# Four edits to a tuned kernel of attention, a gated convolution and DFT mixing: a frequency from a number per token, earlier bits, later sigmoids, other banks

## The chip, the cores and the metric

The kernel runs on one core of a Trainium2 chip. The core has a matrix engine (TensorE, PE in the profile; its weight loads are PEld), VectorE (DVE), ScalarE (ACT) and GpSimd (POOL), each with its own instruction queue, and SyncE (SP), whose queue issues most of the DMAs. The engines meet only at semaphores. The metric is the device time of one execution in microseconds (us).

## The reference, cut to what matters

```python
# 1. attention: 2 batches, 8 heads, 768 tokens, 64 per head
q_bits = (q @ proj > 0); k_bits = (k @ proj > 0)      # 6 bits per token
mask = bucket(q_bits)[..., :, None] == bucket(k_bits)[..., None, :]
scores = where(mask, q @ k.T / 8, -1e9)
x = softmax(scores) @ v                               # -> (2, 768, 512)
# 2. gate: causal convolution of 5 taps per channel
x = (sigmoid(conv(x, conv_w)) * (x @ w_val)) @ w_out
# 3. mixing by DFT along the tokens and along the channels
u = x + real(fft(fft(x, axis=1), axis=2))
un = (u - mean(u)) / sqrt(var(u) + 1e-6)
out = u + maximum(un @ w_ch1, 0) @ w_ch2              # 512 -> 2048 -> 512
```

## The kernel before

Every matmul operand is split into a high and a low part of 32-bit floats, and a product is three matmuls (high x high, high x low, low x high) that add up in one bank of PSUM. The weights arrive as 64-bit floats and are converted on the chip from their two words each (`from64`, `words_split`): masks and shifts on VectorE, a scaling on ScalarE, and at the end a low part (line 156 on GpSimd when `spare`, line 158 on VectorE otherwise) and a high part (line 163, ScalarE). All work stands in each engine's queue in the order of the program; nothing reorders it (`manual_schedule`). A tile waits for the last reader of the memory that it takes over.

**Attention** is a loop over n, 96 blocks of 128 queries (8 pairs of heads, 12 blocks each) and two more steps to drain it. In step n TensorE transposes block n (`p_transpose`), makes the scores of block n + 3 (`scores`) and multiplies with the values for the block pair before (`pv`). VectorE limits the scores (`clamp`, line 549) and makes the low part of the transposed block (`p_low`, line 586); ScalarE does the exponential (`expo`, 556) and the high part (`p_high`, 582). There is one tile of two banks for scores (pool `pss`), so the scores of a block wait for the clamp of the one before; there are two for transposes (`pst`), and one bank each in `psm` and `pso`. `start` prepares the first pair of heads. The second head's projected bits are made by `project(1, ...)` in step 0 and thresholded by `start_bits` (line 440) later in that step; `bits_place` copies them by two DMAs into the operands of the scores.

In the last steps (NT = 96) the value matmuls of the gate for the first half of batch 0 come early (`val_matmul`, line 216, into tiles `early`), the weights of w_out are converted in the gaps, `norm_transpose` (636, 639) turns the reciprocal sums, `x_split` makes the parts of the second half of x, and `sigmoid` makes the gates. A one-element activation (line 878) loads ScalarE's table for sigmoids. `pv_out` of the last block copies its result twice on ScalarE (610, 612), GpSimd adds (615) and multiplies with the norm (696). Then come 48 value matmuls (`late`) and the stage `mixing`.

**Mixing.** The first part finishes the gates, with even and odd sums over the tokens (`even_odd`, line 1002) on VectorE. Then a loop over 12 jobs (batch, symmetry s, block kt) runs through `own` (product with w_out), `fold` (the sum or difference of columns d and 512 - d), `turn` (transposes by TensorE, 1126 and 1128, and their two parts) and `along_d` (the DFT along the channels against `tab`, 1145), each one job behind the other. `fold` leaves the column d = 0 out. So `turn` also transposes the first 128 columns of y, and `along_d` adds two matmuls with a table `first` that is 2 in its row 0 and 0 elsewhere: y[:, 0] reaches all 258 outputs. `both` does the DFT along the tokens (`mixed`, 1165), adds it to y (`total`, 1171 to 1176) and lets GpSimd write u (1186). The centering of batch 0 (`center`) and its transposes stand beside the jobs of batch 1.

**Channel mixing** loops over g, 2 x 16 blocks of 128 of the 2048 hidden channels: `first` (1275) makes the hidden block, `second` (1287) adds to six accumulators `acc0` to `acc5`, one for each block of tokens. For g = 0 and 1 the hidden blocks go through the banks of accumulators 2 to 5. `channel_split(h)` converts half h (w_ch1 for even h, w_ch2 for odd) of block h // 2 and starts the load of half h + 2. Halves 0 and 1 are converted within the mixing, half 2 at the start of the channel mixing.

Of the kernel before, what the change touches and what calls it, by code (L numbers as in the profile page):

```python
# [17 lines left out]
P = 128  # L18
# [30 lines left out]
def dft_tables():  # L49


    d = np.arange(1, DM // 2 + 1)
    l = np.arange(NL)
    ang = 2.0 * np.pi * ((d[:, None] * l[None, :]) % DM) / DM
    cs = 2.0 * np.stack([np.cos(ang), np.sin(ang)], 0)
    cs[0, -1] = 1.0 - 2.0 * (l % 2)
    cs[1, -1] = 0.0
    ch, cl = split12(cs)
    wide = np.stack([ch, cl], 1).reshape(2, 2, 2, P, NL).transpose(3, 0, 1, 2, 4)

    j = np.arange(HS)
    k = np.arange(HS)
    ang = 2.0 * np.pi * ((j[:, None] * k[None, :]) % S) / S
    c = np.cos(ang)
    s = -np.sin(ang)
    c[0, 1::2] = 0.0
    c[1::2, 0] = 0.0
    s[:, 0] = 0.0
    t = np.stack([c, s], 0)
    th, tl = split12(t)  # L70
    seq = np.stack([th, tl], 1).reshape(2, 2, HS // P, P, HS).transpose(3, 0, 1, 2, 4)

    odd = np.zeros((P, 2, P), np.float32)
    odd[0, 0, 1::2] = 1.0
    odd[1::2, 1, 0] = 1.0
    return (
        np.ascontiguousarray(wide, dtype=np.float32),
        np.ascontiguousarray(seq, dtype=np.float32),
        odd,
    )  # L80
# [22 lines left out]
def block_kernel(  # L103
# [23 lines left out]

    def from64(words_of, raw, dst_h, dst_l, half=False, parts=P, spare=False):

        n = raw.shape[1]  # L130
        words = raw.bitcast(I32).rearrange("p (n two) -> p n two", two=2)
        lo, hi = words[:, :, 0], words[:, :, 1]
        a, e, g = (words_of(n, x)[:parts] for x in "aeg")
        b = 4 if half else 3

        def fold(x):
            return x.rearrange("p (c f) -> p c f", c=dst_h.shape[1]) if len(dst_h.shape) == 3 else x

        def s0():
            nc.vector.tensor_scalar(a, hi, 0x7FFFFE00, None, op0=ALU.bitwise_and)  # L140

        def s1():
            nc.scalar.activation(a, a, AF.Relu, scale=8.0, bias=col[:parts, b : b + 1])  # L143

        def s2():
            nc.vector.tensor_scalar(g, hi, 0x1FF, 15, op0=ALU.bitwise_and, op1=ALU.logical_shift_left)
            nc.vector.scalar_tensor_tensor(g, lo, 17, g, op0=ALU.logical_shift_right, op1=ALU.bitwise_or)

        def s3():
            nc.vector.scalar_tensor_tensor(a, hi, -(2 ** 31), a, op0=ALU.bitwise_and, op1=ALU.bitwise_or)  # L150
            nc.vector.tensor_scalar(e, a, -(2 ** 23), None, op0=ALU.bitwise_and)  # L151

        def s4():
            if spare:
                nc.scalar.mul(g.bitcast(F32), g, 2.0 ** -35)
                nc.gpsimd.tensor_tensor(dst_l, fold(g.bitcast(F32)), fold(e.bitcast(F32)), op=ALU.mult)  # L156
            else:
                nc.vector.scalar_tensor_tensor(
                    dst_l, fold(g), 2.0 ** -35, fold(e.bitcast(F32)), op0=ALU.mult, op1=ALU.mult
                )  # L160

        def s5():
            nc.scalar.copy(dst_h, fold(a.bitcast(F32)))

        return [s0, s1, s2, s3, s4, s5]
# [128 lines left out]
    def attention(es):  # L294
# [133 lines left out]
        def two_banks():  # L428
            return [psm.tile([P, HS], F32, tag="m", name="bp"), pso.tile([P, HS], F32, tag="o", name="bp")]
# [86 lines left out]
        def start_bits(bps):  # L516
            bits = st[0]["bits"] = ap1.tile([P, S], F32R, tag="bits", name="bits")
            for a in range(2):
                bit(bits[64:, :], slice(64, P), a, bps)
            bits_place(0, 1)  # L520
            values(0, 1)

# [205 lines left out]
        def conv_weights():  # L728
            cwr, cwh, cwl, cw = cws
            
            def words_of(n, x):
                c0 = (2 + "aeg".index(x)) * P
                return conv_tmp[:, c0 : c0 + n].bitcast(I32)

            steps = from64(words_of, cwr, cwh, cwl, parts=20)
# [33 lines left out]

        tail = []  # L770
        convs = [(b, c, i) for b, c in pairs[: NPR - 1] for i in range(9)]
        start()
        NT = 12 * NPR
        for n in range(NT + 2):
# [6 lines left out]
            if n == 0:  # L781
                bps = project(1, two_banks())
            if n + 3 < NT:
# [19 lines left out]
            if n == 0:  # L803
                start_bits(bps)
            if p + 1 < NPR:
# [10 lines left out]
            if i == (5 if last else 9) and 1 <= p < NPR:  # L816
                norm_mul(p - 1)
            if n == NT - 1:
                xsplit[0, 1] = tuple(
                    ap0.tile([P, R, QB], F32R, tag=x, name="x01").rearrange("p r (c t) -> p (r c t)", c=2)  # L820
# [3 lines left out]
                for c in range(NC):  # L824
                    x_split(0, 1, c, nc.vector)
            if n in (NT - 1, NT):
                norm_transpose(NPR - 1, n - NT + 1)
            if n == NT + 1:
# [40 lines left out]
            if p == 5 and i in (1, 3, 5, 7):  # L869
                x_split(0, 0, i // 2)  # L870
            if NT - 3 <= n < NT + 1:
                c = n - NT + 3
                if c % 2 == 0:
                    early = (pst if c else pss).tile([P, 2, 512], F32, tag="t" if c else "s", name="early")
                tail.append(early[:, c % 2, :HS])
                val_matmul(0, 0, c, tail[c])
            if n == NT - 3:
                nc.scalar.activation(warm, warm, AF.Sigmoid)
            if NT - 2 <= n < NT:
                for x in range(2):  # L880
                    sigmoid(0, 2 * (n - NT + 2) + x)
                if n == NT - 1:
                    g_again(0, slice(0, NC))
            if n >= NT - 2:
                gate(0, 0, n - NT + 2, tail[n - NT + 2])
        out_tile(2)
# [13 lines left out]
    u, mu, uth, utl, rstd = [], [], [], [], []  # L900
    wq, wch, wraw, wst = None, [], {}, []

# [29 lines left out]
    def channel_words(n, x):  # L932
        return wq.tile([P, n], I32, tag=f"cv{x}", name="cv", bufs=1)

    def channel_split(h):
        if h < 2 * NF:
            f, i = divmod(h, 2)
            run(from64(channel_words, wraw[h], *wch[f][2 * i : 2 * i + 2], spare=True))
            channel_load(h + 2)
# [24 lines left out]
    def mixing(es):  # L964
# [11 lines left out]
        tab = mp.tile([P, 2, 2, 2, NL], F32R, name="tab")  # L976
        first = mp.tile([P, NL], F32R, name="first")
        odd = mp.tile([P, 2, P], F32R, name="odd")
# [103 lines left out]
        g_again(1, slice(2, 3))  # L1082
        nc.gpsimd.memset(f32(first), 0.0)
        nc.gpsimd.memset(f32(first)[0:1, :], 2.0)
        for s in range(2):
# [36 lines left out]
        def turn(b, s, kt, part):  # L1122
            n = 2 if part else 3
            pt = bank()
            for i, x in enumerate([folds[b, s, kt, part][:, i * P : (i + 1) * P] for i in range(2)]):
                nc.tensor.transpose(pt[:, i * P : (i + 1) * P], x, ident)
            if n == 3:
                nc.tensor.transpose(pt[:, 2 * P : 3 * P], ys[b, s, kt][:, 0:P], ident)
            fh, fl = turned[b, s, kt, part] = [
                m2.tile([P, 3, P], F32R, tag=f"f{x}", name="ft", bufs=2)[:, :n] for x in "hl"  # L1130
            ]
            src = pt[:, : n * P].rearrange("p (n t) -> p n t", n=n)
            nc.scalar.copy(fh, src)
# [4 lines left out]
        def along_d(b, s, kt, part):  # L1138
            fh, fl = turned[b, s, kt, part]
            ops = [(x[:, i, :], tab[:, part, w, i, :]) for x, w in ((fh, 0), (fh, 1), (fl, 0)) for i in range(2)]  # L1140
            if part == 0:
                ops += [(x[:, 2, :], first) for x in (fh, fl)]
            pa = psum()
# [57 lines left out]
        for i in range(len(jobs) + 2):  # L1201
# [45 lines left out]
    def channel(es):  # L1247
# [9 lines left out]
        for f in order[4:]:  # L1257
            wch[f] = channel_tiles(fp, f)
        channel_split(2)

# [40 lines left out]

        both = []
        for g in range(B * NF + 1):
            if g < B * NF:
# [7 lines left out]
            if g > 0:  # L1312
# [55 lines left out]
```

## Time and profile before

| what | us |
|---|---|
| median of 3 runs | 631.28 (631.07 to 631.45) |
| the profiled execution | 631.46 |
| its span, first to last instruction | 629.7 |
| TensorE busy | 616.0 (98%) |
| VectorE, ScalarE, GpSimd busy | 445.9, 356.4, 263.9 |

The profile is of one execution. The share of an engine's busy time is a mean over stages: attention lies from 0 to 259 us, the mixing to 353, the channel mixing behind it. Times of a row count from the span's start.

### The profile page before, as it was taken

What the parts mean: (1) busy time and instruction counts of PE and PEld (TensorE: products, weight loads), DVE (VectorE), ACT (ScalarE), POOL (GpSimd) and SP (SyncE); (2) the same over time, 40 slices, a digit from 0 to 9 for tenths busy, and PEclk for the clock granted to TensorE, in tenths of its full rate; (3) what the DMA queues carried; (4) which work ended last, traced back from release to release, by engine and by line L of the source; (5) the groups of instructions that cost most, each with busy time, mean ns of one, the idle gap of its engine ahead of it and who ended that gap; (6) DMA issues with size and microseconds to landing.
All of it is one profiled execution on the core that took longest, in us unless ns stands there. A gap on an engine that the chain in (4) does not pass through costs nothing.

```text
span 629.7 us, 10559 instructions
## 1 busy us (share of the span) xinstructions
PE 616.0 (98%) x3794; PEld 576.7 (92%) x3794; DVE 445.9 (71%) x847; ACT 356.4 (57%) x713; POOL 263.9 (42%) x289
## 2 busy tenths in 40 slices
PE   7999999999999999999999899999999999999997
PEld 7899999999999998998899889999998999999996
DVE  5998989898989897797769788889885411111113
ACT  5887989898989797844525255555665111011121
POOL 7133478777888788792350533322331000000000
PEclk9999999999999999999999999999999999999999
DMA  6857585847566530251100144344440200000002
GB/s 155 198 126 169 128 184 123 177 121 167 141 143 158 152 90 13 72 227 68 33 35 1 35 128 132 114 130 134 133 134 1 100 1 1 0 1 1 1 1 100
DMA packets 54060, 60.25 MB, mean 96 GB/s; under 512 B 28936, under 2 KB 42332, under 8 KB 53752
## 3 DMA queue, kind: packets, MB, share of 16 engines
q1 hardware_dynamic: 53272, 56.02, 34.1%
q0 software_dynamic: 432, 3.55, 1.5%
q8 instruction: 30, 0.49, 0.3%
q14 instruction: 22, 0.18, 0.1%
q10 hardware_dynamic: 304, 0.01, 0.0%
HBM read 33.98 MB, written 3.15 MB: 59 GB/s over the span
## 4 chain that ended last, share of the span: by engine, by line
PE 88%; DVE 7%; ACT 2%; issue 1%; DMA 1%; POOL 0%; SPq 0%; DVEq 0%; ACTq 0%; POOLq 0%
PE pf L1275 20%; PE acc L1287 20%; PE sp L537 10%; PE op L597 9%; PE ptp L574 8%; PE ps L1105 5%; PE ps L216 3%; PE ps L1165 3%; PE bp L414 2%; PE ps L1145 2%; DVE ptl L586 2%; DVE sd L549 2%; PE late L216 1%; PE ptp L669 1%; PE ptp L649 1%
## 5 line engine op out<-in xcount | busy, mean ns | idle before, releaser
L1287 PE MATMUL acc<-w,hid 128*128 128x512 f32 x576 | 137.0, 390 | 0.0
L1287 PEld LDWEIGHTS acc<-w,hid 128*128 128x128 f32 x576 | 107.4, 188 | 19.7
L1278 DVE SCALAR_TENSOR_TENSOR hid<-pf,hid 128x384 fp32r<-128x384 f32 x60 | 32.2, 555 | 120.1 <-ACT hid L1277 120.1
L549 DVE TENSOR_SCALAR_CACHE_REDUCE sd<-sp 128x768 f32<-128x768 f32 x96 | 90.9, 948 | 14.7 <-PE sp L537 14.0
L1275 PE MATMUL pf<-uth,w 128*128 128x384 f32 x480 | 94.8, 338 | 0.2 <-POOL w L156 0.2
L586 DVE TENSOR_TENSOR ptl<-ptp,pth 128x768 fp32r<-128x768 f32 x96 | 91.4, 952 | 3.2 <-ACT pth L582 3.2
L537 PE MATMUL sp<-qk 128*128 128x384 f32 x384 | 90.9, 359 | 2.8 <-DVE sd L549 1.5
L1277 ACT ACTIVATE hid<-pf 128x384 fp32r<-128x384 f32 x60 | 28.0, 488 | 113.9 <-PE pf L1275 113.9
L582 ACT CAST pth<-ptp 128x768 fp32r<-128x768 f32 x96 | 77.3, 805 | 26.8 <-PE ptp L574 10.0
L556 ACT ACTIVATE sd<-sd,nm 128x768 f32<-128x768 f32 x96 | 90.7, 945 | 2.7 <-DVE sd L549 2.7
L1275 PEld LDWEIGHTS pf<-uth,w 128*128 128x128 f32 x480 | 85.7, 188 | 2.9 <-POOL w L156 0.6
L156 POOL TENSOR_TENSOR w<-cv 128x512 fp32r<-128x512 f32 x32 | 41.4, 1294 | 89.6 <-DVE cv L151 76.6
L574 PE MATMUL ptp<-ident,sd 128*128 128x128 f32 x576 | 78.6, 272 | 0.2 <-ACT sd L556 0.2
L597 PE MATMUL op<-ptl,v 128*128 128x256 f32 x288 | 73.6, 285 | 0.3 <-DVE ptl L586 0.3
L597 PE MATMUL op<-pth,v 128*128 128x256 f32 x288 | 73.5, 281 | 0.2 <-ACT xc L610 0.2
L537 PEld LDWEIGHTS sp<-qk 128*128 128x128 f32 x384 | 62.4, 189 | 6.4 <-DVE sd L549 3.9
L574 PEld LDWEIGHTS ptp<-ident,sd 128*128 128x128 f32 x576 | 65.9, 141 | 1.1 <-ACT sd L556 0.5
L615 POOL TENSOR_TENSOR xm<-xc,xs 64x256 f32<-64x256 f32 x48 | 35.5, 740 | 68.5 <-DMA xs<-xc 36.0
L597 PEld LDWEIGHTS op<-ptl,v 128*128 128x128 f32 x288 | 54.1, 188 | 1.6 <-DVE ptl L586 0.5
L597 PEld LDWEIGHTS op<-pth,v 128*128 128x128 f32 x288 | 54.2, 188 | 0.6 <-ACT xc L610 0.4
L1275 PE MATMUL pf<-utl,w 128*128 128x384 f32 x240 | 52.1, 338 | 0.0
L143 ACT ACTIVATE cv<-cv,col 128x512 int32<-128x512 int32 x32 | 23.2, 725 | 48.1 <-DVE cv L140 48.1
(214 smaller groups left out, 1047.1 us busy)
## 6 DMA issues: line engine op xcount, KB each, us to landing
raw<-in_moe_w_ch_dram SPq DMA_DIRECT2D x32, 512.0 KB
qk<-ht SPq DMA_DIRECT2D x60, 192.0 KB
qk<-lt SPq DMA_DIRECT2D x30, 192.0 KB
rqk<-in_q_dram SPq DMA_DIRECT2D x16, 192.0 KB
rqk<-in_k_dram SPq DMA_DIRECT2D x16, 192.0 KB
rv<-in_v_dram SPq DMA_DIRECT2D x8, 384.0 KB
out_dram<-o SPq DMA_DIRECT2D x12, 256.0 KB
xs<-xc SPq DMA_DIRECT2D x47, 64.0 KB
```

Source lines behind the costliest of these rows:

```text
L156: nc.gpsimd.tensor_tensor(dst_l, fold(g.bitcast(F32)), fold(e.bitcast(F32)), op=ALU.mult)
L537: nc.tensor.matmul(sp[:, a, :HS], q2[i][:, m, qi * P : (qi + 1) * P], k2[i][:, m, a * HS : (a + 1) * HS], start=m == 1, stop=m == 0,)
L549: nc.vector.tensor_scalar(sd[n].rearrange("p (a c) -> p a c", a=2), sp[:, :, :HS], CLAMP, None, op0=ALU.min, op1=ALU.min, accum_out=st[p][ ...
L556: nc.scalar.activation(sd[n], sd[n], AF.Exp, bias=st[p]["nm"][:, i : i + 1], scale=-1.0, accum_out=st[p]["sums"][:, i : i + 1],)
L574: nc.tensor.transpose(tp[:, r // 3, c0 : c0 + P], sd[n][:, r * P : (r + 1) * P], ident)
L582: nc.scalar.copy(p_parts(n)[0], tp)
L586: nc.vector.tensor_tensor(lo, tp, f32(ho), op=ALU.subtract)
L597: nc.tensor.matmul(po[kb], v3[:, r, c0 : c0 + P], pt[kb][x][:, r, :], start=r == 0 and x == 0, stop=r == R - 1 and x == 1,)
L615: add[kb] = lambda: nc.gpsimd.tensor_tensor(st[p]["xm"][mr, blk * QB : (blk + 1) * QB], xc[mr, :], xs[mr, :], op=ALU.add)
L1275: nc.tensor.matmul(pf[:, :HS], w[:, c, :], x[:, c, cs], start=n == 0, stop=n == 3 * NC - 1)
L1278: nc.vector.scalar_tensor_tensor(hl[:, cs], pf[:, :HS], 0.0, f32(hh)[:, cs], op0=ALU.max, op1=ALU.subtract)
L1287: nc.tensor.matmul(acc, x[:, ts_], w, start=f == 0 and n == 0, stop=f == NF - 1 and n == 2)
```

## The change

1. *d = 0 as a number per token.* The third transpose of `turn`, the table `first` (and the two GpSimd instructions that fill it) and its two matmuls in `along_d` go. Instead the eviction of `along_d` adds y[:, 0] per token: ScalarE's copy becomes an Identity with a bias, VectorE's subtraction an instruction with three operands. A factor of two moves from the table of the channels to those of the tokens.
2. *Second head's bits ahead of a clamp.* In step 0 `start_bits` comes straight behind `project(1, ...)`, ahead of clamp(3). `values(0, 1)` stays where it was.
3. *Sigmoids behind the last copies.* The table load moves from step 93 to 94, the sigmoids of batch 0 from steps 94 and 95 to 95 and 96, the gates with them. In step 95 the early value matmuls and the first `norm_transpose` come ahead of `x_split`.
4. *Banks and first conversion.* Two accumulators are made ahead of the first hidden block, so that all tiles of the channel mixing take other banks. Half 2 of the weights is converted without `spare`: its steps 0 to 2 ahead of `both(1, 0)`, step 3 behind it, the last two at the start of the channel mixing. `from64` asks for its destination only when it writes, since that tile exists only then.

```diff
@@ dft_tables
-    cs = 2.0 * np.stack([np.cos(ang), np.sin(ang)], 0)
-    cs[0, -1] = 1.0 - 2.0 * (l % 2)
+    cs = np.stack([np.cos(ang), np.sin(ang)], 0)
+    cs[0, -1] = 0.5 - (l % 2)
...
-    t = np.stack([c, s], 0)
+    t = 2.0 * np.stack([c, s], 0)
...
-    odd[0, 0, 1::2] = 1.0
-    odd[1::2, 1, 0] = 1.0
+    odd[0, 0, 1::2] = 2.0
+    odd[1::2, 1, 0] = 2.0
@@ start_bits
             bits_place(0, 1)
-            values(0, 1)
@@ attention
+        def val_early(n, early):
+            c = n - NT + 3
+            tail.append(early[:, c % 2, :HS])
+            val_matmul(0, 0, c, tail[c])
...
             if n == 0:
-                bps = project(1, two_banks())
+                start_bits(project(1, two_banks()))
             if n + 3 < NT:
                 clamp(n + 3, scores(n + 3))
...
             if n == 0:
-                start_bits(bps)
+                values(0, 1)
...
             if n == NT - 1:
+                early = pst.tile([P, 2, 512], F32, tag="t", name="early")
+                val_early(n, early)
+                norm_transpose(NPR - 1, 0)
                 xsplit[0, 1] = tuple(
...
-            if n in (NT - 1, NT):
-                norm_transpose(NPR - 1, n - NT + 1)
+            if n == NT:
+                norm_transpose(NPR - 1, 1)
...
-            if NT - 3 <= n < NT + 1:
-                c = n - NT + 3
-                if c % 2 == 0:
-                    early = (pst if c else pss).tile([P, 2, 512], F32, tag="t" if c else "s", name="early")
-                tail.append(early[:, c % 2, :HS])
-                val_matmul(0, 0, c, tail[c])
             if n == NT - 3:
+                early = pss.tile([P, 2, 512], F32, tag="s", name="early")
+            if NT - 3 <= n < NT + 1 and n != NT - 1:
+                val_early(n, early)
+            if n == NT - 2:
                 nc.scalar.activation(warm, warm, AF.Sigmoid)
-            if NT - 2 <= n < NT:
+            if NT - 1 <= n < NT + 1:
                 for x in range(2):
-                    sigmoid(0, 2 * (n - NT + 2) + x)
-                if n == NT - 1:
+                    sigmoid(0, 2 * (n - NT + 1) + x)
+                if n == NT:
                     g_again(0, slice(0, NC))
-            if n >= NT - 2:
-                gate(0, 0, n - NT + 2, tail[n - NT + 2])
+            if n >= NT - 1:
+                for c in range(n - NT + 1, n - NT + (2 if n < NT + 1 else 3)):
+                    gate(0, 0, c, tail[c])
@@ mixing
-        nc.gpsimd.memset(f32(first), 0.0)
-        nc.gpsimd.memset(f32(first)[0:1, :], 2.0)
...
-            if n == 3:
-                nc.tensor.transpose(pt[:, 2 * P : 3 * P], ys[b, s, kt][:, 0:P], ident)
...
-            if part == 0:
-                ops += [(x[:, 2, :], first) for x in (fh, fl)]
...
-            nc.scalar.copy(ah[:, part, slot, :], pa[:, :NL])
-            nc.vector.tensor_tensor(al[:, part, slot, :], pa[:, :NL], f32(ah)[:, part, slot, :], op=ALU.subtract)
+            high, low = ah[:, part, slot, :], al[:, part, slot, :]
+            if part:
+                nc.scalar.copy(high, pa[:, :NL])
+                nc.vector.tensor_tensor(low, pa[:, :NL], f32(high), op=ALU.subtract)
+            else:
+                y0 = ys[b, s, kt][:, 0:1]
+                nc.scalar.activation(high, pa[:, :NL], AF.Identity, bias=y0)
+                nc.vector.scalar_tensor_tensor(
+                    low, pa[:, :NL], y0, f32(high), op0=ALU.add, op1=ALU.subtract
+                )
...
-        for kt in range(3):
+        wnext.extend(channel_steps(2, spare=False))
+        run(wnext.pop(0) for _ in range(3))
+        both(1, 0)
+        wnext.pop(0)()
+        for kt in range(1, 3):
             both(1, kt)
@@ channel
-        channel_split(2)
+        run(wnext)
+        channel_load(4)
...
+        last = [tile_a(t) for t in range(2)]
...
                 if f == 0:
-                    acc = [tile_a(t) for t in range(6)]
+                    acc = (last if b == 0 else [tile_a(t) for t in range(2)]) + [tile_a(t) for t in range(2, 6)]
```

## Rows read from the trace of the kernel before

**Rows 1.** The page's busy time, share of the span and instructions of each engine.

```profile
PE 616.0 (98%) x3794; PEld 576.7 (92%) x3794; DVE 445.9 (71%) x847; ACT 356.4 (57%) x713; POOL 263.9 (42%) x289
```

**Rows 2.** Chain that ended last, 0 to 36 us: start, duration (us), what.

```profile
35.44 0.17 DVE sd L549
```

**Rows 3.** Chain that ended last, whole span.

```profile
377.00 4.24 PE pf L1275 x24
```

**Rows 4.** Timeline, 12 to 40 us: start, duration, engine, line, idle before and its releaser.

```profile
16.60 0.96 DVE L549 TENSOR_SCALAR_CACHE_REDUCE sd<-sp 128x768 f32<-128x768 f32 x1 [1.07 <-PE sp L537]
...
18.45 1.29 DVE L440 TENSOR_SCALAR bits<-bp,col 64x384 fp32r<-64x384 f32 x2
...
19.20 0.55 PE L388 MATMUL tp<-ident,rqk 128*128 128x128 f32 x3 [0.60 <-DVE bits L440]
...
20.80 0.97 PE L537 MATMUL sp<-qk 128*128 128x384 f32 x4 [0.40 <-DVE sd L549]
```

**Rows 5.** Timeline, 246 to 260 us, the end of attention.

```profile
246.13 1.28 ACT L878 ACT_TABLE_LOAD   x1
...
247.53 0.78 ACT L582 CAST pth<-ptp 128x768 fp32r<-128x768 f32 x1
...
250.71 0.37 ACT L278 CAST qk<-cvp 128x256 fp32r<-128x256 f32 x1 [2.05 <-DVE qk L275]
...
251.23 0.52 PE L636 MATMUL rp<-ident,rb 128*128 128x128 f32 x3 [0.65 <-ACT qk L278]
...
255.61 0.55 PE L636 MATMUL rp<-ident,rb 128*128 128x128 f32 x3 [0.45 <-ACT rs L639]
...
258.79 0.86 PE L216 MATMUL late<-x,wvh 128*128 128x384 f32 x4
...
259.44 0.36 ACT L612 COPY xs<-op 64x256 f32<-64x256 f32 x1
```

**Rows 6.** Windows: length, busy us of PE, PEld, DVE, ACT, POOL; clock, DMA share, GB/s.

```profile
250.98:257.64 6.66, 5.62 (x34) 5.19 (x35) 3.85 (x7) 6.63 (x14) 3.75 (x4) 1.00 0.30 91
262.00:284.00 22.00, 22.00 (x128) 22.00 (x127) 20.77 (x37) 11.32 (x25) 20.43 (x24) 1.00 0.50 186
332.00:340.00 8.00, 8.00 (x47) 6.91 (x46) 7.32 (x19) 2.51 (x7) 0.00 (x0) 1.00 0.01 2
```

**Rows 7.** Timeline, 262 to 290 us: start of the mixing.

```profile
262.68 1.02 DVE L1002 TENSOR_TENSOR gt<-g,late 128x384 f32<-128x384 f32 x2 [0.91 <-POOL xT L696]
...
288.63 0.57 ACT L1115 COPY y<-ps 128x512 f32<-128x512 f32 x1
...
289.86 0.41 PE L1126 MATMUL pw<-ident,fold 128*128 128x128 f32 x2
```

**Rows 8.** Groups of TensorE instructions by line and form: busy us, mean ns.

```profile
L1145 PE MATMUL ps<-first,ft 128*128 128x258 f32 x16 | 3.2, 283 | 0.0
...
L1128 PE MATMUL pw<-ident,y 128*128 128x128 f32 x8 | 2.2, 272 | 0.0
```

**Rows 9.** Chain that ended last, 280 to 373 us.

```profile
290.27 0.11 PE pw L1128
...
293.19 0.98 PE ps L1145 x8
```

**Rows 10.** Groups of ScalarE instructions by line.

```profile
L1316 ACT ACTIVATE u<-u,mu 128x512 f32<-128x512 f32 x12 | 8.6, 717 | 0.0
```

**Rows 11.** Timeline, 343 to 376 us: from the mixing to the channel mixing.

```profile
349.27 7.88 POOL L1186 TENSOR_TENSOR u<-y 128x512 f32<-128x512 f32 x6 [22.07 <-DVE y L1176]
...
354.05 1.64 PE L1275 MATMUL acc<-uth,w 128*128 128x384 f32 x8 [0.94 <-DVE y L1176]
354.48 1.51 DVE L146 TENSOR_SCALAR cv<-raw 128x512 int32<-128x512 int32 x1
...
360.33 0.97 PE L1275 MATMUL acc<-uth,w 128*128 128x384 f32 x4 [0.32 <-POOL w L156]
...
360.69 0.42 DVE L146 TENSOR_SCALAR cv<-raw 128x512 int32<-128x512 int32 x1
```

More of the change, by code (lines that the diff above doesn't have):

```diff
@@ L126, in pool, with from64 @@
         return es.enter_context(tc.tile_pool(name=name, bufs=bufs, reuse_waits="tile", **kw))
-    def from64(words_of, raw, dst_h, dst_l, half=False, parts=P, spare=False):
+    def from64(words_of, raw, dst, half=False, parts=P, spare=False):
         n = raw.shape[1]
@@ L136, in fold @@
         def fold(x):
-            return x.rearrange("p (c f) -> p c f", c=dst_h.shape[1]) if len(dst_h.shape) == 3 else x
+            shape = dst()[0].shape
+            return x.rearrange("p (c f) -> p c f", c=shape[1]) if len(shape) == 3 else x
         def s0():
@@ L155, in s4 @@
                 nc.scalar.mul(g.bitcast(F32), g, 2.0 ** -35)
-                nc.gpsimd.tensor_tensor(dst_l, fold(g.bitcast(F32)), fold(e.bitcast(F32)), op=ALU.mult)
+                nc.gpsimd.tensor_tensor(dst()[1], fold(g.bitcast(F32)), fold(e.bitcast(F32)), op=ALU.mult)
             else:
                 nc.vector.scalar_tensor_tensor(
-                    dst_l, fold(g), 2.0 ** -35, fold(e.bitcast(F32)), op0=ALU.mult, op1=ALU.mult
+                    dst()[1], fold(g), 2.0 ** -35, fold(e.bitcast(F32)), op0=ALU.mult, op1=ALU.mult
                 )
         def s5():
-            nc.scalar.copy(dst_h, fold(a.bitcast(F32)))
+            nc.scalar.copy(dst()[0], fold(a.bitcast(F32)))
         return [s0, s1, s2, s3, s4, s5]
@@ L733, in words_of @@
                 return conv_tmp[:, c0 : c0 + n].bitcast(I32)
-            steps = from64(words_of, cwr, cwh, cwl, parts=20)
+            steps = from64(words_of, cwr, lambda: (cwh, cwl), parts=20)
             def whole():
@@ L900, in block_kernel @@
     u, mu, uth, utl, rstd = [], [], [], [], []
-    wq, wch, wraw, wst = None, [], {}, []
+    wq, wch, wraw, wst, wnext = None, [], {}, [], []
     def late_tiles():
@@ L933, in channel_words, with channel_steps @@
         return wq.tile([P, n], I32, tag=f"cv{x}", name="cv", bufs=1)
+    def channel_steps(h, spare=True):
+        f, i = divmod(h, 2)
+        return from64(channel_words, wraw[h], lambda: wch[f][2 * i : 2 * i + 2], spare=spare)
     def channel_split(h):
@@ L937, in channel_split @@
             f, i = divmod(h, 2)
-            run(from64(channel_words, wraw[h], *wch[f][2 * i : 2 * i + 2], spare=True))
+            run(channel_steps(h))
             channel_load(h + 2)
@@ L976, in mixing @@
         tab = mp.tile([P, 2, 2, 2, NL], F32R, name="tab")
-        first = mp.tile([P, NL], F32R, name="first")
         odd = mp.tile([P, 2, P], F32R, name="odd")
@@ L1122, in turn @@
         def turn(b, s, kt, part):
-            n = 2 if part else 3
             pt = bank()
@@ L1126, in turn @@
                 nc.tensor.transpose(pt[:, i * P : (i + 1) * P], x, ident)
-            if n == 3:
-                nc.tensor.transpose(pt[:, 2 * P : 3 * P], ys[b, s, kt][:, 0:P], ident)
             fh, fl = turned[b, s, kt, part] = [
-                m2.tile([P, 3, P], F32R, tag=f"f{x}", name="ft", bufs=2)[:, :n] for x in "hl"
+                m2.tile([P, 2, P], F32R, tag=f"f{x}", name="ft", bufs=2) for x in "hl"
             ]
-            src = pt[:, : n * P].rearrange("p (n t) -> p n t", n=n)
+            src = pt[:, : 2 * P].rearrange("p (n t) -> p n t", n=2)
             nc.scalar.copy(fh, src)
```

## The prediction

> **What bounds the kernel now.** I read the page first: TensorE is busy 98% of the span [rows 1], so time can only go where its work shrinks or where it waits. Then the chain of waits, which is TensorE almost throughout, and the timeline at each place where it is not. There are four: the first scores, the end of attention, the start of the mixing by DFT (`mixing`), and the hand-over to the channel mixing. Between the first and the second the chain leaves TensorE again only for short visits such as that at 35.44 [rows 2]; from 377 us on it alternates two TensorE lines [rows 3], so nothing that happens earlier on the other engines is seen there. The change touches all four places and, besides, takes matmuls out.
>
> **First scores (`start_bits` moved).** VectorE was free from 15.53 to 16.60, 1.07 us, waiting for scores(3). The two bits instructions, 1.29 us together, came only at 18.45, after clamp(3) and p_low(0), and so clamp(4) started at 19.78 and scores(5) at 20.80. TensorE also waited 0.60 us at 19.20, because the transposes of the next pair use the bank that the bits read [rows 4]. Moved, the bits run from 15.53 to about 16.82, clamp(3) starts 0.22 us later than before, and p_low(0) ends at about 18.67. scores(4) follows clamp(3), which ends at 16.60 + 0.22 + 0.96 = 17.78; four score matmuls take 0.97, so clamp(4) can start at about 18.85, 0.93 us earlier than before, and scores(5) with it. After 20.80 both engines run on without a break, and VectorE has its bits behind it too, so the gain travels on; the VectorE visit at 35.44 [rows 2] moves with it, as its work is the same and starts earlier. The two DMAs of `bits_place` now stand in SP's queue ahead of nothing that is waited for: they are issued some 1.3 us earlier, which helps scores(6). values(0,1) keeps its place on GpSimd. Ends: nothing (if a load holds the next pair) and 1.29 (all bits hidden). I take **-0.9**.
>
> **End of attention (sigmoids behind the copies).** Before, the load of the sigmoid table, 1.28 us at 246.13, stands ahead of the copy pth(94), which starts only at 247.53. All that depends on it (p_low(94), the last weight conversion, its copy at 250.71) is late; so are the pair of sigmoids and pth(95) behind it. TensorE pays with 0.65 us at 251.23, 0.45 at 255.61 and more at the mixed waits between [rows 5]. After the change pth(94) can start where the load stood, 1.4 us earlier. Of that I pass on 1.2 (VectorE has its own work between): the weight copy starts at about 249.5, the table load follows it (0.3 + 1.28 + 0.2 for the small activation), and pth(95) starts at about 251.3. The early value matmuls go ahead of the first norm transpose, so TensorE no longer waits for that bank, nor at the second transpose. The two waits are 1.10 us by their rows; with the restart around each and the mixed waits I put TensorE's gain at 1.5 to 2.0 and go on with the upper end, which is harder for my forecast: the first late value matmul at about 256.8, not 258.79 [rows 5].
>
> But the other engines are not. From 250.98 to 257.64 ScalarE is busy 6.63 of 6.66 us [rows 6], and all of that (four sigmoids, four copies of x, two of the norm, pth, xc) stands as before ahead of the last copies xc and xs in its queue. It now starts at 251.3 and has to wait some 0.8 us for the norm transpose, since TensorE now does that behind twelve value matmuls. So 251.3 + 6.66 + 0.8 + 0.4 for xc puts xs at about 259.1, against 259.44 [rows 5]: 0.3 to 0.5 us earlier. On xs hang GpSimd's last sum and the multiplication by the norm, and on that, by its 0.91 us of waiting, VectorE's gt at 262.68 [rows 7]. From there VectorE has no pause: 20.77 of the 22 us to 284 are busy, the 1.23 that is missing being the wait for gt and overheads [rows 6]. At its end stand the table load, y at 288.63 and the fold, for which TensorE's transpose at 289.86 waits [rows 7]. Today the two chains meet there almost exactly. If TensorE comes 2.0 us earlier and VectorE 0.4, TensorE stands still there for about 1.6 us: the stall is moved, not removed. I take **-0.4**; the ends are 0 and -2.0.
>
> **d = 0 as a number per token.** 16 matmuls of 258 columns with `first` and 8 transposes go [rows 8]. Eight matmuls take 0.98 us, so 0.1225 each, and a transpose 0.11 [rows 9]: 16 x 0.1225 + 8 x 0.11 = 2.84 us. The two GpSimd memsets were off the path, with GpSimd's queue emptied before TensorE came to the stage. ScalarE's copy becomes an Identity with a bias; such an instruction on 512 columns takes 0.72 us [rows 10], and ScalarE is idle for two thirds of 332 to 340 [rows 6]; VectorE's subtraction becomes one of three operands, like the last sums at about the same cost. The copies behind the transposes shrink by a third. Not all of the 2.84 can be kept: in the second batch the centering of the first runs on VectorE, which is busy 7.32 of the 8 us from 332 to 340 [rows 6] and loses only the third of four small instructions. Of the 0.70 us that TensorE saves behind job 7 (two transposes and two pairs of matmuls, 0.22 + 0.49), I let it keep 0.15. Ends: -2.84, and -1.42 if the whole second batch is VectorE's. I take **-2.3**.
>
> **Hand-over (banks and first conversion).** TensorE's first matmul of the channel mixing waits 0.94 us for the last sum y (line 1176): its accumulator took the bank which that sum still read. Then it needs the second block's weights, whose conversion VectorE begins only after the sums. From 354.05 to 360.33 it does 28 matmuls [rows 11], which at the later pace of 24 in 4.24 us [rows 3] would be 4.95 us; the stretch took 6.28, so 1.33 is lost, and with 0.94 the loss is **2.3 us**. With two accumulators taken first, the opening matmuls move to two other banks; only a bank read by one of the last two sums could hold them, at up to the same 0.94. The conversion's first four VectorE instructions now run ahead of the sums of kt 0 and two more behind them, where TensorE works on matmuls that need no sum. The sums then run late, which nobody waits for once the banks differ. The last part, one VectorE instruction instead of one on ScalarE and one on GpSimd, comes behind all sums. The load of the next raw weights is freed earlier by this.
>
> A price is hidden here. Beside GpSimd's six u (7.88 us from 349.27) the conversion's line 146 took 1.51 us, and 0.42 at 360.69 without them [rows 11]: 1.1 us more each. Two of the moved instructions fall into that stretch, and the last one may. The two would put 1.1 + 2.2 = 3.3 us between the sums; VectorE waits between them anyway, for about half of that, so I let the last sum end some 1.7 us after its 354.0 of before, and the last instruction, 0.7 + 1.1 us, at about 357.5 on the old clock. It is wanted at 353.1 + 28 x 0.177 = 358.05, so by the rows 0.5 is spare and the sum stays -2.3. *The Trainium skill, SBUF — State Buffer, Who interferes with whom, says that GpSimd and VectorE (in a two-port mode or with two SBUF inputs) hold a shared port pair exclusively for a whole instruction, and that the one that starts first blocks the other fully. The trace agrees that VectorE is blocked (1.51 against 0.42). By the rule one more lost turn is possible, and the time is then that of the second rival.* I take **-2.3**; the ends are -0.6 (0.94 kept in another bank and 0.8 lost to one more addition, below) and -2.6 (the last weight wait of the rows, 0.32, counted double).
>
> **Sum.** Against the profiled execution's 631.46 us (span 629.7 and 1.8 around it): -0.9 - 0.4 - 2.3 - 2.3 = -5.9, so 625.6; the median of the runs shown, 631.28, is 0.18 lower, so **625.4**.
>
> **Rivals.**
> - *The end of attention keeps its 2.0 us* (chance 0.13). For it: TensorE's rows name waits of its own here, and the other queues may come sooner than I place them. Against: ScalarE's 6.63 of 6.66 us [rows 6]. Time: 625.4 - 1.6 = 623.8.
> - *VectorE becomes the bound around the conversion* (0.17): its last instruction loses one more turn to an addition, 7.88 / 6 = 1.31 us, and ends at 358.8, so that TensorE waits 0.8; and the second batch's saving goes (+0.9). For it: 7.32 of 8 us busy [rows 6] and 1.51 for 0.42 [rows 11]. Against: the 4.95 us of matmuls ahead of the need [rows 3]. Time: 625.4 + 1.7 = 627.1.
> - *The change of banks or the early bits do nothing* (0.12): the opening matmuls meet a late sum in the new bank (+0.9), or the start's gain dies at a load (+0.9). For it: two of the six banks hold the late sums. Time: 626.3, both 627.2.
> - *Slower than before* (0.03): Identity with a bias needs another ScalarE table than its neighbours, so that each of 8 evictions loads one and the next copy loads back, 8 x 2 x 1.28 us [rows 5] = 20.5 us on ScalarE. It decides from about 30% of that exposed to TensorE (6 us); half exposed gives 635.6. Against: line 1316 runs this very form behind the square root at a mean of 717 ns, which holds no load [rows 10].
>
> My forecast has 0.55. Under it alone the time is 624.6 to 626.3. To leave out no more than 2 in 10, the range takes in the first three rivals: **623.6 to 627.7**. A measurement of this kernel tells about 0.2%, 1.3 us, from no change; every case but the last is faster by more, and I leave some for mishaps I don't see: faster 0.93, same 0.04, slower 0.03.
>
> **What would show it.** Right: scores(5) at about 19.9 and no wait for bits; the table load behind the weight copy; first late matmul at about 255.9 and, new, a TensorE wait of over 1 us for the first fold; eight transposes and 16 matmuls fewer in the mixing; no wait of the first channel matmul for y, none for the second block's weights. Wrong: no new wait at the first fold (then the time is near 624), waits for w or y at the hand-over, table loads beyond three.

## The result and the profile after

| | before | after |
|---|---|---|
| median of four executions each, us | 631.27 (631.07 to 631.45) | 625.54 (624.55 to 625.94) |
| the profiled execution | 631.46 | 624.55 |
| its span | 629.7 | 622.8 |

The ratio is 0.9907 (95% interval 0.989 to 0.9924), a gain of 5.7 us where 5.9 was forecast. A second measurement of the same kernel (run after_again below) gave 626.01 us and 0.9918 (0.9904 to 0.9931). The profiled execution of after is its fastest, which matters below.

The page of after, its first part, against [rows 1]: TensorE's busy time fell by 4.9 us, the rest of the span by 2.0.

```profile
PE 611.1 (98%) x3770; PEld 572.7 (92%) x3770; DVE 444.1 (71%) x848; ACT 355.5 (57%) x712; POOL 263.0 (42%) x286
```

The timeline of after, first scores (start, duration, engine, line, idle before and its releaser), against [rows 4].

```profile
15.26 1.29 DVE L444 TENSOR_SCALAR bits<-bp,col 64x384 fp32r<-64x384 f32 x2
...
16.58 0.96 DVE L552 TENSOR_SCALAR_CACHE_REDUCE sd<-sp 128x768 f32<-128x768 f32 x1
...
17.60 0.97 PE L540 MATMUL sp<-qk 128*128 128x384 f32 x4 [0.69 <-DVE sd L552]
18.41 0.49 PE L392 MATMUL tp<-ident,rqk 128*128 128x128 f32 x3
...
18.61 0.96 DVE L552 TENSOR_SCALAR_CACHE_REDUCE sd<-sp 128x768 f32<-128x768 f32 x1
```

The bits stand where VectorE was idle, and the transposes at 18.41 no longer wait for them. The next scores start at 19.63 instead of 20.80; this execution's first score matmul was already 0.31 earlier (10.48 against 10.79), so the move is worth 0.86.

The timeline of after at the end of attention, against [rows 5]; behind it the window of [rows 6].

```profile
248.32 0.37 ACT L282 CAST qk<-cvp 128x256 fp32r<-128x256 f32 x1 [1.73 <-DVE qk L279]
...
248.71 1.28 ACT L888 ACT_TABLE_LOAD   x1
...
250.11 0.78 ACT L585 CAST pth<-ptp 128x768 fp32r<-128x768 f32 x1
...
255.78 0.86 PE L220 MATMUL late<-x,wvh 128*128 128x384 f32 x4
...
257.91 0.36 ACT L615 COPY xs<-op 64x256 f32<-64x256 f32 x1
```

```profile
250.98:257.64 6.66, 6.66 (x45) 6.50 (x44) 5.13 (x9) 5.87 (x13) 4.38 (x4) 1.00 0.29 92
```

TensorE has no idle time left in it (6.66 of 6.66, before 5.62). Its first late matmul comes 3.01 us earlier than before, but the copy xs only 1.53 earlier. Of both, 1.13 came from the start of this execution. So the edit itself gave TensorE 1.88 and the other engines 0.40. What became of the difference stands 30 us further on, in the timeline of after against [rows 7]:

```profile
261.15 1.02 DVE L1016 TENSOR_TENSOR gt<-g,late 128x384 f32<-128x384 f32 x2 [0.78 <-POOL xT L699]
```

```profile
285.70 1.28 ACT L1109 ACT_TABLE_LOAD   x1
287.00 0.20 ACT L1109 ACTIVATE warm<-warm 128x1 f32<-128x1 f32 x1
287.10 0.57 ACT L1127 COPY y<-ps 128x512 f32<-128x512 f32 x1
287.76 0.42 DVE L1130 TENSOR_TENSOR fold<-ps,y 128x256 f32<-128x256 f32 x1 [0.97 <-issue]
...
288.33 0.41 PE L1137 MATMUL pw<-ident,fold 128*128 128x128 f32 x2 [1.63 <-DVE fold L1130]
```

gt, y and the fold are all earlier by the same 1.53 as xs: the chain is rigid. Its last link is ScalarE's, since VectorE stands idle for 0.97 us ahead of the fold until y, behind the table load, is there. TensorE waits 1.63 us for its end; the row of the kernel before shows no such wait.

The groups of after that take the place of [rows 8, 9] (mean ns of one behind the busy us), and the window at the centering, as in the last line of [rows 6] but on the new clock:

```profile
L1163 DVE SCALAR_TENSOR_TENSOR a<-ps,y,a 128x258 fp32r<-128x258 f32 x8 | 3.8, 480 | 3.3 <-ACT a L1162 3.3
L1162 ACT ACTIVATE a<-ps,y 128x258 fp32r<-128x258 f32 x8 | 3.8, 478 | 14.8 <-PE ps L1152 12.9 <-issue 1.9
```

```profile
328.90:336.90 8.00, 8.00 (x49) 6.99 (x48) 7.68 (x20) 2.88 (x9) 0.00 (x0) 1.00 0.00 0
```

The Identity with a bias takes 0.48 us where a copy takes 0.37, and there are three table loads in all, as before. TensorE stays full although VectorE is busy 7.68 of 8 us.

The timeline of after at the hand-over, against [rows 11]:

```profile
345.11 0.68 DVE L154 SCALAR_TENSOR_TENSOR cv<-raw,cv 128x512 int32<-128x512 int32 x1
...
345.33 3.04 POOL L1202 TENSOR_TENSOR u<-y 128x512 f32<-128x512 f32 x2 [21.21 <-DVE y L1192]
...
345.82 1.40 DVE L155 TENSOR_SCALAR cv<-cv 128x512 int32<-128x512 int32 x1
...
348.69 1.56 PE L1296 MATMUL acc<-uth,w 128*128 128x384 f32 x8
...
349.46 0.41 DVE L1192 SCALAR_TENSOR_TENSOR y<-ps,y 128x255 f32<-128x255 f32 x1
349.79 0.74 DVE L162 SCALAR_TENSOR_TENSOR w<-cv 128x512 fp32r<-128x512 int32 x1
```

```profile
357.08 4.29 PE L1308 MATMUL acc<-w,hid 128*128 128x512 f32 x18
361.20 0.87 PE L1296 MATMUL pf<-uth,w 128*128 128x384 f32 x4
362.31 0.96 PE L1296 MATMUL pf<-uth,w 128*128 128x384 f32 x4 [0.23 <-POOL w L160]
```

The first matmul of the channel mixing starts at 348.69 without a wait, while the last sum runs until 349.87. Only 0.23 us of weight wait is left, for the third block; the kernel before had 0.2 us there too.

### The profile page after: what moved, and what is told of

Its sections match the earlier page's. It is cut to its first block, busy times and chain, and to the rows that moved or that the text cites. A ratio compares the mean times of both kernels' runs of the same rounds, so it can differ in the third digit from the quotient of the medians.

```text
span 622.8 us, 10510 instructions
## 1 busy us (share of the span) xinstructions
PE 611.1 (98%) x3770; PEld 572.7 (92%) x3770; DVE 444.1 (71%) x848; ACT 355.5 (57%) x712; POOL 263.0 (42%) x286
## 4 chain that ended last, share of the span: by engine, by line
PE 84%; DVE 11%; issue 1%; ACT 1%; DMA 1%; POOL 1%; SPq 0%; DVEq 0%; POOLq 0%; ACTq 0%
PE pf L1296 20%; PE acc L1308 20%; PE sp L540 10%; PE op L600 10%; PE ptp L577 8%; PE ps L1117 4%; PE ps L1181 3%; PE bp L418 2%; DVE sd L552 2%; DVE ptl L589 2%; PE ps L1152 1%; PE ptp L672 1%; PE early L220 1%; DVE pw L248 1%; PE acc L1296 1%
## 5 line engine op out<-in xcount | busy, mean ns | idle before, releaser
L160 POOL TENSOR_TENSOR w<-cv 128x512 fp32r<-128x512 f32 x31 | 40.1, 1293 | 87.0 <-DVE cv L155 73.0
L239 POOL TENSOR_TENSOR g<-g,conv_tmp 128x768 f32<-128x768 f32 x27 | 46.5, 1722 | 1.2
```

Source lines behind the costliest of these rows:

```text
L160: nc.gpsimd.tensor_tensor(dst()[1], fold(g.bitcast(F32)), fold(e.bitcast(F32)), op=ALU.mult)
L239: nc.gpsimd.tensor_tensor(dst, dst, tmp, op=ALU.add)
```

## Experiments

Stages are compared by the starts of TensorE's first instruction of each line in the profiled executions. A: first score matmul to first early value matmul. B: on to the first late one. C: on to the first fold's transpose. D: on to the first matmul of `mixed`. E: on to the first of the channel mixing. F: on to its first second-layer matmul.

| run | median us | ratio to before (95%) | A | B | C | D | E | F |
|---|---|---|---|---|---|---|---|---|
| before | 631.27 | | 232.27 | 15.73 | 31.07 | 25.13 | 39.06 | 9.85 |
| after | 625.54 | 0.9907 (0.989, 0.9924) | 231.45 | 13.85 | 32.55 | 23.55 | 36.81 | 8.39 |
| after_again | 626.01 | 0.9918 (0.9904, 0.9931) | 232.52 | 13.85 | 32.58 | 23.55 | 36.77 | 8.39 |
| d0_alone | 628.9 | 0.9959 (0.9948, 0.9971) | 232.42 | 15.74 | 31.05 | 23.55 | 37.87 | 9.81 |
| bits_alone | 630.8 | 0.9996 (0.9987, 1.0006) | 232.38 | 15.72 | 31.06 | 25.12 | 39.06 | 9.92 |
| sigm_alone | 631.18 | 0.9997 (0.9988, 1.0005) | 232.36 | 13.87 | 32.55 | 25.12 | 39.07 | 9.85 |
| hand_alone | 628.89 | 0.9957 (0.9944, 0.997) | 232.39 | 15.74 | 31.07 | 25.13 | 38.00 | 8.39 |
| no_banks | 626.25 | 0.9921 (0.9909, 0.9934) | 231.35 | 13.83 | 32.59 | 23.57 | 38.15 | 8.39 |
| no_conv | 627.87 | 0.9948 (0.9935, 0.996) | 232.34 | 13.86 | 32.55 | 23.58 | 36.81 | 11.03 |
| taps_out | 622.92 | 0.9867 (0.9851, 0.9882) | 232.26 | 13.86 | 30.76 | 23.54 | 36.82 | 8.31 |
| cw_early | 626.24 | 0.9913 (0.9899, 0.9927) | 233.02 | 13.86 | 32.57 | 23.56 | 36.79 | 8.39 |
| table_moved | 624.43 | 0.9884 (0.9869, 0.99) | 231.95 | 13.84 | 31.51 | 23.57 | 36.79 | 8.38 |
| fold_first | 625.36 | 0.9892 (0.9875, 0.991) | 232.12 | 13.83 | 30.76 | 23.54 | 38.15 | 8.46 |
| best | 625.72 | 0.9907 (0.9893, 0.9921) | 233.07 | 13.84 | 30.76 | 23.55 | 38.14 | 8.39 |

Stages B to F repeat within 0.15 us wherever an edit leaves them alone. Stage A does not, and that is the subject of the third group.

### One part of the change at a time

**d0_alone**: the kernel before with part 1 of the change only (tables, `turn`, `along_d`).

```diff
-            if part == 0:
-                ops += [(x[:, 2, :], first) for x in (fh, fl)]
...
+                nc.scalar.activation(high, pa[:, :NL], AF.Identity, bias=y0)
```

> Only the edit of d = 0 is made on the kernel before. Theory (the parts add up, each held by the engine that the prediction named): 16 matmuls and 8 transposes less, of which nearly all is kept: 2.3 to 2.8 us faster, about 628.7. Rival (VectorE is the bound in the second batch, where the centering runs): at most 1.4 us faster, 629.9.

D lost 1.58 and E 1.19 us, 2.77 together of the 2.84 of removed matmuls: the theory, at its upper end.

**bits_alone**: part 2 only.

```diff
             if n == 0:
-                bps = project(1, two_banks())
+                start_bits(project(1, two_banks()))
```

> Only the second head's bits move, on the kernel before. Theory: scores(5) comes 0.9 us earlier and that travels to the end: 630.4. Rival (a load or a later engine holds the next steps, so the start's gain is given back): 631.3, no change.

The median of the 12 executions is 0.63 us under that of the kernel before beside them (631.43), between theory and rival, and the interval of the ratio takes in no change. Eight lie from 629.92 to 630.91 and four from 631.7 to 632.89. The profiled one (632.62) is of the second group: its first score matmul starts 1.06 us later than in the kernel before, and its A has no gain. No trace shows the first group, so this run leaves open how often the gain is kept.

**sigm_alone**: part 3 only.

```diff
             if n == NT - 3:
+                early = pss.tile([P, 2, 512], F32, tag="s", name="early")
+            if NT - 3 <= n < NT + 1 and n != NT - 1:
+                val_early(n, early)
+            if n == NT - 2:
                 nc.scalar.activation(warm, warm, AF.Sigmoid)
```

> Only the sigmoids, the table load, the early value matmuls and the first norm transpose move, on the kernel before. Theory (VectorE's chain from the last copies to the first fold sets the end of the stage): TensorE comes 1.8 us earlier to the late value matmuls and then stands still 1.5 us or more ahead of the first fold's transpose; 0.4 us faster, 630.9. Rival (TensorE's own waits are the loss): 1.8 us faster, 629.5, and no new wait.

B lost 1.86 and C gained 1.48, with the new wait of 1.6 us for the fold, as in the theory: 0.38 net, too small for the median to tell from nothing.

**hand_alone**: part 4 only.

```diff
+        wnext.extend(channel_steps(2, spare=False))
+        run(wnext.pop(0) for _ in range(3))
...
+        last = [tile_a(t) for t in range(2)]
```

> Only the banks and the first conversion change, on the kernel before. Theory: the first channel matmul does not wait for the last sum and the second block's weights are there in time: 2.3 to 2.6 us faster, about 628.8. Rival (GpSimd's additions block the conversion until after the need): 1.2 us faster, 630.1, with a wait for w in the second block.

E lost 1.06, F 1.46, together 2.52: the theory.

### The two halves of the hand-over, and the late chain

**after_again**: the changed kernel once more, beside the next three.

> The changed kernel once more, beside the runs of this call. If the four parts add up, it is 5.5 to 6.5 us faster than the kernel before, 625 to 626; its trace again shows a wait of some 1.6 us for the first fold. If the profile seen first was lucky (its first transposes took 0.86 us where the kernel before took 1.51), the span here is 0.3 us or more longer.

The gain was 5.2 us against the kernel before beside it (631.22), a little under the range. The wait for the first fold is there again (C 32.58), and the span is 1.4 us longer than in the first profile, 624.2. So the execution profiled first was a lucky one, by 1.07 us in A and 0.29 ahead of it.

**no_banks**: the changed kernel, its accumulators taken as before.

```diff
-        last = [tile_a(t) for t in range(2)]
...
-                    acc = (last if b == 0 else [tile_a(t) for t in range(2)]) + [tile_a(t) for t in range(2, 6)]
+                    acc = [tile_a(t) for t in range(6)]
```

> The changed kernel without the two accumulators made ahead. Theory: the first channel matmul again waits for the last sum, which now comes about 1 us behind the last DFT matmul; 1.0 us slower than the changed kernel. Rival (the banks alone are worth nothing once the weights come early): no change.

TensorE's waits of this run from 345 to 352 us (engine, tile and line, what it waited for, total, times, longest):

```profile
PE acc L1296 <- DVE y L1192: 1.2, 1, 1.2
```

E is 1.38 longer than after_again's, more than the 0.94 of [rows 11]; that the conversion makes the sums later fits this. The median is only 0.24 above after_again's, too little to tell, and the profiled execution, the run's fastest, has an A 1.17 shorter than after_again's. So the theory stands on stage E, not on the median.

**no_conv**: the changed kernel, the conversion behind the mixing as before.

```diff
-        wnext.extend(channel_steps(2, spare=False))
...
-        run(wnext)
-        channel_load(4)
+        channel_split(2)
```

> The changed kernel with the second block's first half converted at the start of the channel mixing, as before, but with the new banks. Theory: the opening matmuls start 1 us earlier, and all of that is waited again for the weights, so the whole gain of the hand-over is lost: 2.3 to 2.6 us slower than the changed kernel. Rival (the banks carry their own 0.9 us): 1.4 to 1.7 us slower.

Its waits from 345 to 362 us:

```profile
PE acc L1283 <- ACT w L163: 1.8, 1, 1.8
```

E keeps its gain and F grows by 2.64, as the theory has it. The median is 1.86 above after_again's, between theory and rival. Against d0_alone (E 37.87, F 9.81), the banks alone gain 37.87 + 9.81 - 36.81 - 11.03 = -0.16 us, that is nothing, and the conversion alone (no_banks: E 38.15, F 8.39) 1.14; both, in after, 2.48. The halves uncover each other: a TensorE that starts earlier waits longer for the same weights.

**taps_out**:

```diff
-        for kk in range(5):
+        for kk in range(3):
             x, w = xT[1][:, 3, kk + a * HS : kk + (a + 1) * HS], cwt[:, kk, 3:4]
```

> The changed kernel with two of the five taps of the late convolution left out (channels 384 to 511 of batch 1), four VectorE instructions of 0.65 us between the last copies and the first fold. Theory (VectorE's chain makes TensorE wait 1.6 us there): the wait goes and the time falls by 1.6 us. Rival (TensorE or another queue is the bound): no change.

C fell to 30.76, and the wait for the fold is gone. So VectorE's taps are on the chain to the first fold, and the stall is 32.58 - 30.76 = 1.8 us; 31.07 - 30.76 = 0.3 of it the kernel before had too. The rest of the median's 3.1 lies not in B to F.

**table_moved**: the changed kernel, the Sqrt table loaded at step 7 of the mixing.

```diff
-        nc.scalar.activation(warm, warm, AF.Sqrt)
...
             elif i == 7:
                 both(0, 2)
+                nc.scalar.activation(warm, warm, AF.Sqrt)
```

> The load of the Sqrt table is moved from ahead of the last gates' use to behind the third pair of first matmuls of the channel's hand-over at step 7. Theory (ScalarE's queue, with 1.28 us of table load in it, has a share in the lateness of the first fold): the first fold's transpose comes up to 1.0 us earlier and the median lies 0.5 to 1.0 us lower, 624.6 to 625.4. Rival (VectorE's chain of the late taps and the gates alone sets the first fold): the wait of 1.6 us before the first transpose stays and the median is 625.5 to 626.0.

C is 1.04 shorter, as the theory has it, and the wait of 1.6 became this (waits of TensorE, 255 to 300 us):

```profile
PE pw L1136 <- DVE fold L1129: 0.6, 1, 0.6
```

So ScalarE's load ahead of y was part of the chain. It is the fastest version that computes everything: 624.43 us, where the changed kernel had 625.54 and 626.01. The interval of its ratio overlaps with that of the first; stage C is the firmer evidence.

**fold_first**: table_moved, and the last gates behind the first fold.

```diff
+            if i == 0:
+                late_gates()
```

(`late_gates` holds the second sigmoid of the late convolution and the four gates that stood ahead of the loop.)

> As the run with the table moved, and the second half's sigmoid of the late convolution with the four gates of the second head are put behind the first fold. Theory (the wait of 1.6 us before the first fold's transpose is VectorE's order: gates that nobody needs yet stand ahead of the fold): the wait goes, the stretch from the first late matmul to the first transpose falls from 32.55 to about 31.0, and the median lies 1.6 us lower, 624.0 to 624.4. Rival (the gates come late for the next folds and stop TensorE there): the wait goes at the first transpose and comes back before the third or the fourth, and the median stays within 0.3 us of 625.5 to 626.0.

C is at its floor of 30.76, but E went back to 38.15, with the wait of no_banks (waits of TensorE, 300 to 372 us):

```profile
PE acc L1305 <- DVE y L1198: 1.2, 1, 1.2
```

The rival was right that a wait would come back, though not in its place: the opening matmuls met the bank of the last sum again. That the later gates change the order in which the banks come free is my reading of it; no run tested it.

### Where the start's gain goes

In after_again VectorE's clamps run 0.31 us behind after's until the eighth, and 1.71 behind at the ninth. First the timeline of after from 27.8 to 29.2 us, then of after_again:

```profile
27.82 0.20 DVE L150 TENSOR_SCALAR conv_tmp<-cwr 20x128 int32<-20x128 int32 x1
...
28.07 0.28 DVE L151 SCALAR_TENSOR_TENSOR conv_tmp<-cwr,conv_tmp 20x128 int32<-20x128 int32 x1
...
28.27 0.27 DVE L154 SCALAR_TENSOR_TENSOR conv_tmp<-cwr,conv_tmp 20x128 int32<-20x128 int32 x1
...
28.58 0.21 DVE L155 TENSOR_SCALAR conv_tmp<-conv_tmp 20x128 int32<-20x128 int32 x1
...
28.72 0.94 DVE L552 TENSOR_SCALAR_CACHE_REDUCE sd<-sp 128x768 f32<-128x768 f32 x1
...
29.14 0.74 POOL L618 TENSOR_TENSOR xm<-xc,xs 64x256 f32<-64x256 f32 x1 [13.05 <-DMA xs<-xc]
```

```profile
28.00 0.74 POOL L618 TENSOR_TENSOR xm<-xc,xs 64x256 f32<-64x256 f32 x1 [11.63 <-DMA xs<-xc]
...
28.14 0.68 DVE L150 TENSOR_SCALAR conv_tmp<-cwr 20x128 int32<-20x128 int32 x1
...
28.71 0.51 POOL L172 TENSOR_SCALAR v<-rv 128x384 fp32r<-128x384 f32 x1
...
28.85 0.50 DVE L151 SCALAR_TENSOR_TENSOR conv_tmp<-cwr,conv_tmp 20x128 int32<-20x128 int32 x1
...
29.28 0.27 DVE L154 SCALAR_TENSOR_TENSOR conv_tmp<-cwr,conv_tmp 20x128 int32<-20x128 int32 x1
29.30 1.13 POOL L382 TENSOR_TENSOR v<-rv,v 128x384 fp32r<-128x384 f32 x1
...
29.59 0.92 DVE L155 TENSOR_SCALAR conv_tmp<-conv_tmp 20x128 int32<-20x128 int32 x1
...
30.43 0.94 DVE L552 TENSOR_SCALAR_CACHE_REDUCE sd<-sp 128x768 f32<-128x768 f32 x1
...
31.43 0.44 PE L540 MATMUL sp<-qk 128*128 128x384 f32 x1 [0.83 <-DVE sd L552]
```

Four tiny instructions convert the convolution's weights. They start 17.3 to 17.4 us behind the first score matmul in both executions. In after GpSimd's sum of xs starts 18.66 behind it, and they are through. In after_again it starts at 17.23, and three of the four last until the GpSimd instruction beside them ends (28.74, 29.22, 30.43), 1.4 us more in all. The fourth, line 154, starts 0.02 ahead of the GpSimd instruction beside it and takes its 0.27. *The Trainium skill, SBUF — State Buffer, Who interferes with whom, says that between GpSimd and a VectorE instruction (in a two-port mode, or with two SBUF inputs beside a GpSimd read) whichever issues first keeps the shared port pair for its whole instruction while the other is fully blocked; the trace agrees, within 0.13 us, at all three ends.*

All profiles but the two with another order of the conversion fall in line (us behind the first score matmul):

| kernels | GpSimd's sum | ninth clamp | A |
|---|---|---|---|
| late bits, sum behind the conversion: sigm_alone, before, hand_alone, d0_alone | 19.44 to 20.22 | 19.20 to 19.23 | 232.27 to 232.42 |
| early bits, sum behind it: no_banks, after | 18.56, 18.66 | 18.25, 18.24 | 231.35, 231.45 |
| early bits, sum within it: fold_first, table_moved | 17.61, 17.70 | 18.98, 18.99 | 232.12, 231.95 |
| early bits, sum ahead of it: taps_out, bits_alone, no_conv, after_again | 16.96 to 17.23 | 19.39 to 19.66 | 232.26 to 232.52 |

So the early bits are worth 0.96 us at the ninth clamp where the conversion is left alone, and nothing where it is held.

**cw_early**: the changed kernel with that conversion one step earlier.

```diff
-CW = (2, 3, 4, 4, 5, 6, 7, 12)
+CW = (2, 2, 3, 3, 5, 6, 7, 12)
```

> The conversion of the convolution's weights (tiny instructions on VectorE, 20 partitions) is put one step earlier: its parts come at steps 2, 2, 3, 3 in place of 2, 3, 4, 4, so that the four instructions that stood beside GpSimd's add of xs and its values (28.0 to 31 us) lie ahead of them. Theory (the first scores' gain of 0.9 us is given back at the ninth clamp, in executions in which the DMA of xs lands before these four instructions and GpSimd's work keeps them off the port: 0.68, 0.50, 0.27 and 0.92 us in place of 0.20, 0.28, 0.27 and 0.21): the four take about 0.2 to 0.28 us each wherever xs lands, the stretch from the first score matmul to the first early matmul is 231.4 us in the profile, and the median lies 0 to 0.9 us under the changed kernel's 625.5 to 626.0, with less spread. Rival (the give-back comes from elsewhere, the clamps themselves beside GpSimd): the stretch stays at 232.3 to 232.5 and the median at 625.5 to 626.0.

The first half of the theory held: with the sum at 28.06 the four took 0.20, 0.28, 0.27 and 0.21. But A became 233.02. The ScalarE part of the conversion, now straight behind its VectorE part, stood still in ScalarE's queue. The timeline of cw_early:

```profile
23.36 0.20 DVE L144 TENSOR_SCALAR conv_tmp<-cwr 20x128 int32<-20x128 int32 x1
...
23.60 0.40 ACT L147 ACTIVATE conv_tmp<-conv_tmp,col 20x128 int32<-20x128 int32 x1 [1.02 <-DVE conv_tmp L144]
...
23.91 0.77 ACT L585 CAST pth<-ptp 128x768 fp32r<-128x768 f32 x1
24.72 0.96 DVE L589 TENSOR_TENSOR ptl<-ptp,pth 128x768 fp32r<-128x768 f32 x1 [0.27 <-ACT pth L585]
...
26.38 0.62 DVE L398 SCALAR_TENSOR_TENSOR lt<-tp,col,ht 128x384 fp32r<-128x384 f32 x1 [0.71 <-ACT ht L397]
```

ScalarE waited 1.02 us, the copy pth behind it came late, and VectorE waited for that and for the next copy; the clamp behind them, the eighth, came 1.94 later than in after_again. One give-back was exchanged for another: at the ninth clamp the two kernels are again within 0.3 us of each other. The 0.50 by which A is longer than after_again's arises between the ninth and the eleventh; its cause stays open. The median, 626.24, lies above what theory and rival said.

**best**: fold_first with cw_early's order.

> The two edits together: gates behind the first fold, table moved, and the convolution's weights converted one step earlier. Theory (the two give-backs lie in stretches apart and add up): 1.6 and up to 0.9 us, a median of 623.1 to 624.4. Rival (one of them is taken up by the wait for the first value matmuls or the next fold): 624.4 to 625.5.

Both faults came along: A 233.07, E 38.14. At 625.72 us, above theory and rival, it is no better than the changed kernel; table_moved is.

## Why the prediction was right, and where it was not

The time was within 0.2 us of the first median. By its terms, measured as stages:

| term | predicted | measured |
|---|---|---|
| first scores | -0.9 | -0.82 in after's profile, +0.25 in after_again's |
| end of attention | -0.4 | -1.88 + 1.48 = -0.40 |
| d = 0 | -2.3 | -2.77 |
| hand-over | -2.3 | -2.52 |

- *First scores.* The mechanism was right to the clamp (0.86 of 0.93 us at the next scores), and the step "both engines run on without a break, ... so the gain travels on" failed. Four steps further on, in six of the eight profiles with early bits and the old place of the conversion, GpSimd's sum comes to where VectorE converts, and all or most of the gain is lost there. The other three terms, stages B to F, sum to -5.69, and the medians fell by 5.73 and 5.21: in the median of the changed kernel the start brought almost nothing. Its rival had the right sign and another place: not a load, but VectorE held beside GpSimd. The prediction also read the chain too short: the view that it cites ends at 36 us, and from the visit at 35.44 on, the chain of the kernel before stays on VectorE until 46.68. The gain was not lost there, though: in after this stretch begins 1.29 and ends 1.28 us earlier.
- *End of attention.* Right in mechanism and size, TensorE's 1.9 us and the 1.5 that come back at the first fold. The rival that keeps 2.0 us fell with sigm_alone and taps_out. The table load on ScalarE, which the prediction named only as standing at the end of that chain, is worth 1.04 of the stall; the chain that it put on VectorE runs through both engines. "Almost exactly" hid the 0.3 us that TensorE already lost there.
- *d = 0.* The mechanism was right, the reserve of 0.55 for VectorE mis-sized: 0.07 was lost. TensorE stayed full while VectorE was busy 7.68 of 8 us; that is not yet a bound.
- *Hand-over.* Right; the 0.94 of the bank measured 1.06 in stage E, the 1.33 of the weights 1.46 in F. The instruction beside GpSimd's sums took 1.40 us as feared, but only one did, and the last part was through at 349.79 + 0.74 = 350.53, 3.1 us ahead of the 29th matmul, which wants it at 348.69 + 28 x 0.177 = 353.65. The second rival (VectorE the bound) fell.
- *Slower by table loads* fell: three loads as before, and 0.48 us an Identity.

The total was right partly by luck, because errors cancelled: the start's missing 0.9 against 0.47 and 0.22 more from the two others.

## What to carry to other kernels

When an engine gets its work earlier at one place, follow the other engines' queues to the next place where all chains meet; the gain there is that of the slowest chain, and no more. Two edits at one hand-over are costed together, since the first wait removed uncovers the second. A gain at the start of a long pipelined stretch is sure only if the timing of the DMAs and of GpSimd beside VectorE stays as it was, so profile more than one execution before you believe in half a microsecond.

## What the runs showed of the hardware that was not expected

- VectorE instructions on only 20 partitions, of 0.20 to 0.28 us, are held like large ones until the GpSimd instruction beside them ends: they took 0.68, 0.50 and 0.92 us.
- Stages of the same code repeat to 0.15 us between executions, except the first 232 us, which differ by 1.07 in two executions of one kernel (231.45 and 232.52) by the moment at which GpSimd's sum starts, which is released by a DMA. Why that DMA lands 1.4 us earlier or later relative to the first scores was not tried. The first score matmul itself starts between 10.12 and 11.85 us in the fourteen profiles.
